# Attention and two gated layers on one core: a planner that knows the port of DVE and POOL, attention outputs on halves of PE's columns, and an opening time for the second chunk's attention

## The chip, the cores and the metric

One core of a Trainium2 chip. The time is that of one launch on the device, in microseconds (us). The engines are PE (matrix products), ACT (scalar), DVE (vector), POOL (GpSimd) and SP (the queue from which the transfers are started). Each engine carries out its instructions in the order in which the program lists them for that engine.

## The reference, cut to what matters

Random-feature attention over 4 batches of 576 tokens and 8 heads of 64, then two gated layers of width 512 with 1536 hidden units, over all 2304 tokens:

```python
def phi(x):                      # x already scaled by 64 ** -0.25
    h = einsum('bhsd,md->bhsm', x, omega) - sum(x * x) / 2
    return exp(h - max(h)) / sqrt(128)
q_p, k_p = phi(q_s), phi(k_s)
kv = einsum('bhsm,bhsd->bhmd', k_p, v); z = sum(k_p, over tokens)
attn = einsum('bhsm,bhmd->bhsd', q_p, kv) / (einsum('bhsm,bhm->bhs', q_p, z) + 1e-6)
x = heads side by side                       # 2304 x 512
x = (silu(x @ w_gate) * (x @ w_val)) @ w_out       # first layer
x = ((x @ w_a) * (x @ w_b)) @ w_out2               # second layer
```

The kernel takes the weights as 64-bit floats and makes 32-bit ones of them.

## The kernel before, in words

The tokens are cut into five chunks (`spans`): chunks 0 to 3 of 512 and chunk 4 of 256. Heads go in pairs, p = 0 to 3. For each chunk c, `layer(c, 0)` and `layer(c, 1)` do the two gated layers, and beside them the attention of chunk c + 1 is done (`keys` and `queries`, lines 833 to 837), so that PE has both kinds of work to choose from. Chunk 0's attention comes alone, at the start.

In the layers each number x is split in two fp32r parts, a high one (made by ACT, an ACTIVATE copy) and a low one (DVE, `sub`, line 321: x minus the high part). A product of 128 x 128 weights with 512 tokens is three matmuls, lines 770, 771, 772: high x high, high weights x low tokens, low weights x high tokens. `weights` loads a tile of 128 x 512 weights; the first time it makes 32-bit floats of 64-bit ones with two ACT instructions (lines 729, 732) and two DVE instructions (lines 735, 738), and keeps the result in DRAM; each time ACT makes the high part `wh` (line 750) and DVE the low part `wl` (line 753, counted at line 321). `put` (line 528) turns a PSUM tile into the high and low parts `xh`, `xl` of a layer's input.

Attention. `features` (line 367) projects with omega, takes the maximum (DVE, line 453), and the exponential (ACT, line 465). The squares of the tokens are made by POOL (line 382), their sums by DVE (384, 387: `s`, `nsq`), and `top` and `bias` are DVE's too (456, 460). `how` says in which form: WHOLE (chunk 0, plain fp32), SPLIT (chunk 1, three fp32r matmuls, line 443), STACKED (chunks 2 to 4, line 418). Then chunks 0 and 1 take `own` (line 556): transposes (567), outputs with the denominator as a 65th column (587), a division on DVE (604, 608, 612: `xt`), transposes back (621), `put`. Chunks 2 to 4 take `shared` (line 627): denominators from POOL products (652) and DVE sums (659), POOL scales the features (669), PE transposes them for each head h (679), and then they are split: ACT makes `fh` (682), DVE `fl` (685, counted at 321). For each batch b that the chunk touches, ACT and DVE split the sums `kvs` of both heads into high and low parts in a tile `kp` (693, 696) that holds 64 columns of head 0, 64 zeros, 64 columns of head 1; POOL writes the zeros once (354). `attend` (line 700) does, for each head, three matmuls (705) with 128 columns of `kp`, half of them zeros, all six adding up in one PSUM tile. A chunk of 512 touches two batches (widths 128 and 384 in chunk 2, 320 and 192 in chunk 3), chunk 4 touches one: five calls for each head pair, 20 in all, 120 matmuls.

Order. No order is written by hand. Each operation is recorded with its engine, a cost (`pace` for how long it holds the engine, `lat` for when its result is there) and a due time (`on`, line 316; `act`, `dve`, `pool`, `pe`, `dma` are the costs). `Plan.order` (line 98) then plays a list schedule: at each step the engine that is free first takes, of its operations whose inputs and tiles are there, the one that is due first; the order in which they are taken is the order in which each engine's instructions are issued. An operation that is due late is taken early if its engine has nothing else ready. `slack` makes an engine's inputs later in the plan, `after` is an earliest time. Tiles come from rings (`Ring`): a tile is given out again when all operations on its last use are planned. Four tiles of the ring `zb` lie in the memory of `fT`, which `own` uses. The costs do not know of each other: an instruction of DVE costs the same whether POOL works beside it or not.

Of the kernel before, what the change touches and what calls it, by code (L numbers as in the profile page):

```python
# [16 lines left out]
P = 128  # L17
# [4 lines left out]
class Ring:  # L22


    def __init__(self, make, n, name):
        self.tiles = [make(f"{name}{i}") for i in range(n)]
        self.free = [(0.0, i) for i in range(n)]
        self.recorded = []
        self.next = 0
# [22 lines left out]
class Op:  # L52
    __slots__ = ("eng", "pace", "lat", "due", "fn", "table", "deps", "bufs", "users", "open",
                 "ready", "start", "end", "n", "size", "slack")


class Plan:

# [10 lines left out]
    RATE = 0.24  # L69

# [3 lines left out]
    def add(self, eng, pace, due, fn, reads=(), writes=(), lat=None, table=None, size=0.0, slack=0.0,  # L74
            after=0.0):
        o = Op()
        o.eng, o.pace, o.due, o.fn, o.table, o.size, o.slack = eng, pace, due, fn, table, size, slack
        o.lat, o.ready = pace if lat is None else lat, after
# [19 lines left out]
    def order(self):  # L98
# [11 lines left out]
        table, pipe, done = None, 0.0, []  # L110

# [21 lines left out]
        while True:  # L133
# [18 lines left out]
            pace, lat = o.pace, o.lat  # L152
            if o.table and o.table != table:
# [24 lines left out]
            for b in o.bufs:  # L178
                b.left -= 1
                b.end = max(b.end, o.end)  # L180
                if b.left == 0 and b.ring is not None:
                    b.ring.free.append((b.end, b.slot))
                    for x in held.pop(id(b.ring), []):
                        offer(x)
# [11 lines left out]
def attention_moe_moe(ctx: ExitStack, tc: tile.TileContext, qT, kT, q, k, v, omegaT,  # L196
# [23 lines left out]
    NT = 512  # L220
# [33 lines left out]
    zeros = Fixed(None)  # L254
# [21 lines left out]
    r_zb = ring("zb", 2, [P, 2, M])  # L276
    for i in range(NT // P):
        r_zb.free.append((0.0, len(r_zb.tiles)))
        r_zb.tiles.append(r_fT.tiles[0].rearrange("p h (t m) -> p (h t) m", m=M)[:, 2 * i:2 * i + 2])
    r_kp = ring("kp", 2, [P, 2, 3, D], F32R)  # L280
    r_fh = ring("fh", 2, [P, NT], F32R)
    r_fl = ring("fl", 2, [P, NT], F32R)
# [31 lines left out]
    slack = dict.fromkeys((PE, ACT, DVE, POOL, SP), 0.0)  # L314

    def on(eng, cost, due, fn, reads=(), writes=(), table=None, late=None, after=0.0):
        return plan.add(eng, due=due, fn=fn, reads=reads, writes=writes, table=table,
                        slack=slack[eng] if late is None else late, after=after, **cost)
# [8 lines left out]
    n_ffn = 3 * (2 * NF * KD + NF * KD)  # L327
    begin = [ALONE]
# [8 lines left out]
    def constants():  # L337
# [15 lines left out]
        for i, t in enumerate(r_kp.tiles):  # L353
            on(POOL, dict(pace=0.25), 60, lambda t=t: nc.gpsimd.memset(
                t[:, :, 1].bitcast(F32), 0.0), writes=[(zeros, i)], after=ALONE)
        on(DVE, dve(256), 30, lambda: nc.vector.tensor_copy(bdh.tile, bd.tile),
           reads=[(bd, *bd.state)], writes=[(bdh,)], after=ALONE / 2)
        on(DVE, dve(256), 30, lambda: sub(nc.vector, bdl.tile, bd.tile, bdh.tile),
# [8 lines left out]
    def features(rT, tok, nt, step, f, due, length, how, psum, first):  # L367
# [19 lines left out]
        on(DVE, dve(16), due - 2, lambda: nc.vector.tensor_scalar(  # L387
# [21 lines left out]
        for g in range(0, nt, 2):  # L409
# [46 lines left out]
            on(DVE, dve(4), d, lambda mx=mx, top=top, n=n, g=g: nc.vector.scalar_tensor_tensor(  # L456
# [3 lines left out]
            on(DVE, dve(4), d, lambda top=top, bias=bias, n=n, g=g: nc.vector.tensor_tensor(  # L460
# [166 lines left out]
    def shared(c, p, f, due, length):  # L627
# [9 lines left out]
        for g in range(0, nt, 2):  # L637
# [25 lines left out]
            on(DVE, dve(4), d, lambda g=g: nc.vector.tensor_scalar(  # L663
# [10 lines left out]
        for h in range(2):  # L674
            d = due + length * (0.5 + 0.2 * h)
            ps, fh, fl = ps_t.buf(), r_fh.buf(), r_fl.buf()
            turned.append((fh, fl))
            for t in range(nt):
# [3 lines left out]
            on(ACT, act(n, 0, True), d, lambda ps=ps, fh=fh: nc.scalar.activation(  # L682
                out=fh.tile[:, 0:n], in_=ps.tile[:, 0:n], func=AF.Copy),
                reads=[(ps, *range(nt))], writes=[(fh,)])
            on(DVE, dve(n), d, lambda ps=ps, fh=fh, fl=fl: sub(
                nc.vector, fl.tile[:, 0:n], ps.tile[:, 0:n], fh.tile[:, 0:n]),
                reads=[(ps, *range(nt)), (fh,)], writes=[(fl,)])
        ps = ps_t.buf()
        for b in batches:
            kp, kv = r_kp.buf(), sums[b, p]  # L690
            cols = slice(max(t0, b * S) - t0, min(t1, (b + 1) * S) - t0)
            width = cols.stop - cols.start
            on(ACT, act(2 * D), due + length * 0.3, lambda kp=kp, kv=kv: nc.scalar.activation(
                out=kp.tile[:, 0, 0:3:2], in_=kv.tile[:, :, 0:D], func=AF.Copy),
                reads=[(kv, 0), (zeros, *range(2))], writes=[(kp, 0)])
            on(DVE, dve(2 * D), due + length * 0.3, lambda kp=kp, kv=kv: sub(
                nc.vector, kp.tile[:, 1, 0:3:2], kv.tile[:, :, 0:D], kp.tile[:, 0, 0:3:2]),
                reads=[(kv, 0), (kp, 0), (zeros, *range(2))], writes=[(kp, 1)])
            for h in range(2):
                def attend(h=h, kp=kp, cols=cols):  # L700
                    (xh, xl), out = turned[h], ps.tile[:, cols]
                    hi, lo = (kp.tile[:, i].rearrange("p a d -> p (a d)")[:, D * h:D * h + P]
                              for i in range(2))
# [176 lines left out]
```

## Time and profile before

| what | us |
|---|---|
| median of 3 runs (lowest, highest) | 1060.49 (1054.83, 1061.13) |
| the profiled execution's own time | 1058.15 |
| its span, from first to last instruction | 1056.4 |
| busy time of PE | 1039.0 |
| busy time of DVE | 748.8 |
| busy time of ACT | 686.6 |
| busy time of POOL | 170.4 |

The profile is of one execution. Durations in it are of single instructions; a matmul's duration reaches past the start of the next one, so what matmuls cost in a row is read from the distance of their starts. An idle time is named with the engine that ended it.

### The profile page before, as it was taken

Reading aid. Unit: us, or ns where it says so; the run is one execution under the profiler, and the core shown is the slowest. Engines: PE = TensorE matmul, PEld = TensorE weight load, DVE = VectorE, ACT = ScalarE, POOL = GpSimd, SP = SyncE. Lnnn points to the kernel's source line nnn. Section 1 sums busy time; section 2 is a strip of 40 time slices with the busy share of each in tenths; the row PEclk is TensorE's granted clock in tenths of the full one; section 3 lists DMA queues with packets and bytes.
Section 4 is the critical chain, followed back from the end, with each engine's and each line's share of the span. In section 5 each row is a group of like instructions: output and inputs, shape, how many; then the busy total and the mean of one; then the engine's idle time right before and its main releaser. Section 6 shows DMA issues by size and latency. Waiting matters only on the chain.

```text
span 1056.4 us, 15912 instructions
## 1 busy us (share of the span) xinstructions
PE 1039.0 (98%) x5444; PEld 887.8 (84%) x5444; DVE 748.8 (71%) x1441; ACT 686.6 (65%) x1433; POOL 170.4 (16%) x148
## 2 busy tenths in 40 slices
PE   7989999999999999999999999999999999999998
PEld 6877888888888878888888888888888888889998
DVE  5989899999766698998544577775554365537663
ACT  5988788888666767887444567665564255437563
POOL 1321020220200042343200034223000011000000
PEclk9999999999999999999999999999999999999999
DMA  7856877687865465564433333333333332336663
GB/s 246 280 188 218 254 259 229 222 257 227 287 201 182 159 216 174 181 205 147 130 104 96 100 113 106 89 87 114 99 100 100 90 92 88 100 120 186 184 182 99
DMA packets 102768, 172.02 MB, mean 163 GB/s; under 512 B 9376, under 2 KB 42784, under 8 KB 102688
## 3 DMA queue, kind: packets, MB, share of 16 engines
q1 hardware_dynamic: 102608, 170.99, 52.0%
q8 instruction: 42, 0.69, 0.3%
q14 instruction: 38, 0.31, 0.1%
q10 hardware_dynamic: 80, 0.03, 0.0%
HBM read 147.39 MB, written 23.59 MB: 162 GB/s over the span
## 4 chain that ended last, share of the span: by engine, by line
PE 87%; DVE 7%; ACT 3%; issue 2%; DMA 1%; SPq 0%; DVEq 0%; ACTq 0%
PE ps_m L771 26%; PE ps_m L772 26%; PE ps_m L770 26%; PE ps_kv L497 3%; PE ps_p L418 2%; PE ps_p L443 1%; PE ps_t L705 1%; DVE w L738 1%; DVE wl L321 1%; PE ps_t L587 1%; DVE mx L453 1%; PE ps_t L679 1%; DVE w L735 1%; PE ps_m L443 1%; DVE h L791 0%
## 5 line engine op out<-in xcount | busy, mean ns | idle before, releaser
L321 DVE TENSOR_TENSOR wl<-w,wh 128x512 fp32r<-128x512 f32 x360 | 262.8, 734 | 170.3 <-ACT wh L750 164.3
L770 PE MATMUL ps_m<-xh,wh 128*128 128x512 f32 (+1 forms) x960 | 359.4, 374 | 1.5 <-ACT wh L750 0.8
L771 PE MATMUL ps_m<-xl,wh 128*128 128x512 f32 (+1 forms) x960 | 355.4, 370 | 2.9 <-DVE xl L321 2.9
L772 PE MATMUL ps_m<-xh,wl 128*128 128x512 f32 (+1 forms) x960 | 355.1, 370 | 0.0
L750 ACT ACTIVATE wh<-w 128x512 fp32r<-128x512 f32 x360 | 224.9, 629 | 129.5 <-PE ps_m L771 99.6
L772 PEld LDWEIGHTS ps_m<-xh,wl 128*128 128x128 f32 x960 | 181.8, 189 | 31.5 <-DVE wl L321 0.7
L771 PEld LDWEIGHTS ps_m<-xl,wh 128*128 128x128 f32 x960 | 181.7, 189 | 30.0 <-DVE xl L321 3.6
L770 PEld LDWEIGHTS ps_m<-xh,wh 128*128 128x128 f32 x960 | 181.8, 189 | 29.1 <-ACT wh L750 1.3
L770 PE MATMUL ps_m<-hh,wh 128*128 128x512 f32 (+1 forms) x480 | 180.8, 377 | 0.0
L772 PE MATMUL ps_m<-hh,wl 128*128 128x512 f32 (+1 forms) x480 | 177.3, 369 | 0.0
L771 PE MATMUL ps_m<-hl,wh 128*128 128x512 f32 (+1 forms) x480 | 177.2, 369 | 0.0
L321 POOL TENSOR_TENSOR rs<-xT,rs 64x576 fp32r<-64x576 f32 (+4 forms) x48 | 63.7, 1327 | 536.2 <-issue 203.7
L791 DVE TENSOR_TENSOR h<-a,ps_m 128x512 f32<-128x512 f32 (+1 forms) x120 | 75.5, 629 | 51.6 <-PE ps_m L772 42.4
L788 ACT ACTIVATE a<-ps_m 128x512 f32<-128x512 f32 (+1 forms) x120 | 66.3, 552 | 66.9 <-PE ps_m L772 66.5
L772 PEld LDWEIGHTS ps_m<-hh,wl 128*128 128x128 f32 x480 | 90.5, 189 | 15.6
L770 PEld LDWEIGHTS ps_m<-hh,wh 128*128 128x128 f32 x480 | 90.7, 189 | 12.5
L771 PEld LDWEIGHTS ps_m<-hl,wh 128*128 128x128 f32 x480 | 90.7, 189 | 12.0
L794 ACT ACTIVATE hh<-h 128x512 fp32r<-128x512 f32 (+1 forms) x120 | 70.6, 588 | 32.2 <-DVE h L791 30.1
L735 DVE SCALAR_TENSOR_TENSOR w<-w 128x512 uint32<-128x512 uint32 x108 | 78.1, 726 | 7.1 <-ACT w L732 6.8
L321 DVE TENSOR_TENSOR hl<-h,hh 128x512 fp32r<-128x512 f32 (+1 forms) x120 | 77.3, 644 | 6.1 <-ACT hh L794 2.7
L738 DVE SCALAR_TENSOR_TENSOR w<-w,w 128x512 uint32<-128x512 uint32 x108 | 78.0, 723 | 2.6 <-ACT w L729 2.5
L732 ACT ACTIVATE w<-w 128x512 uint32<-128x512 uint32 x108 | 72.5, 678 | 5.7 <-DMA w<-w 5.6
(92 smaller groups left out, 1055.1 us busy)
## 6 DMA issues: line engine op xcount, KB each, us to landing
w<-kept SPq DMA_DIRECT2D x252, 256.0 KB, 2.7
w<-w SPq DMA_DIRECT2D x108, 512.0 KB, 4.6
kept<-w SPq DMA_DIRECT2D x72, 256.0 KB, 4.5
kt<-k_t SPq DMA_DIRECT2D x16, 320.0 KB, 3.8
vt<-v_t SPq DMA_DIRECT2D x16, 320.0 KB, 4.6
xT<-kT SPq DMA_DIRECT2D x16, 288.0 KB, 4.0
qt<-q_t SPq DMA_DIRECT2D x16, 256.0 KB, 4.1
outT<-h SPq DMA_DIRECT2D x16, 256.0 KB, 2.1
```

Of the source, the lines that this page charges most:

```text
L321: eng.tensor_tensor(out=out, in0=a, in1=hi.bitcast(F32), op=ALU.subtract)
L497: nc.tensor.matmul(kv.tile[:, (P + 1) * h:(P + 1) * (h + 1)], lhsT=f.tile[0:r, t, h], rhs=vt.tile[0:r, t], start=(t == 0 and h == 0), stop ...
L732: on(ACT, act(CW), due - 10, lambda: nc.scalar.activation(out=raw.tile[:, :, 0], in_=raw.tile[:, :, 0], func=AF.Copy, scale=0.875 * 2.0 ** ...
L735: on(DVE, dve(CW), due - 9, lambda: nc.vector.scalar_tensor_tensor(out=raw.tile[:, :, 0], in0=raw.tile[:, :, 1], scalar=0x80000000, in1=ra ...
L738: on(DVE, dve(CW), due - 9, lambda: nc.vector.scalar_tensor_tensor(out=w.tile.bitcast(U32), in0=w.tile.bitcast(U32), scalar=3, in1=raw.til ...
L750: on(ACT, act(CW), due - 7, lambda: nc.scalar.activation(out=hi.tile.rearrange("p a c -> p (a c)"), in_=w.tile, func=AF.Copy), reads=[(w,) ...
L770: nc.tensor.matmul(o, lhsT=hi.tile[:, wi], rhs=a, start=first, stop=False)
L771: nc.tensor.matmul(o, lhsT=hi.tile[:, wi], rhs=b, start=False, stop=False)
L772: nc.tensor.matmul(o, lhsT=lo.tile[:, wi], rhs=a, start=False, stop=last)
L788: on(ACT, act(n, 0, True), due, lambda a=a, ps=ps: nc.scalar.activation(out=a.tile[:, 0:n], in_=ps[0].tile[:, 0:n], func=AF.Silu if m == 0 ...
L791: on(DVE, dve(n), due, lambda a=a, h=h, ps=ps: nc.vector.tensor_tensor(out=h.tile[:, 0:n], in0=a.tile[:, 0:n], in1=ps[1].tile[:, 0:n], op= ...
L794: on(ACT, act(n), due + 2, lambda h=h, hh=hh: nc.scalar.activation(out=hh.tile[:, 0:n], in_=h.tile[:, 0:n], func=AF.Copy), reads=[(h,)], w ...
```

## The change: what it does

Five edits.

- The planner gets a shared port for DVE and POOL (`HELD`). Operations marked `port=True` are all of POOL's that go by `pool` and those of DVE with two inputs in SBUF, and some small ones (`dve(n, True)`). When a marked operation's turn comes while the other engine holds the port, its planned pace and latency grow by the wait; DVE takes an unmarked operation instead if it has one. This changes planned times and so the order on every engine; the instructions of `weights`, `layer` and `features` stay as they are.
- `shared` no longer splits the features: ACT copies each head's transposed features to a plain fp32 tile `ft` (ring of 3), and DVE's `fl` goes. `kp` goes, with its zeros, its ACT and its DVE instructions.
- `attend` is one operation for both heads: an fp32 matmul for each head, with the 64 columns of that head's sums as weights and its output on partitions 0 to 63 or 64 to 127 of the PSUM tile. The planner's cost of it is new. `put` then waits for all batches' parts.
- `OPENS = 55.0`: the operations of chunk 1's attention on PE, ACT, DVE and POOL (not SP's loads) may start no earlier than 55 us in the plan.
- `r_zb`'s four tiles inside `fT` are free only once `fT` has had its last use in the plan (`heir`).

```diff
-    def dve(n, rate=1):
-        return dict(pace=0.07 + n / 960 / rate, lat=0.19 + n / 960 / rate)
+    def dve(n, port=False):
+        return dict(pace=0.07 + n / 960, lat=0.19 + n / 960, port=port)
     def pool(n):
-        return dict(pace=0.2 + n * 0.0023)
+        return dict(pace=0.2 + n * 0.0023, port=True)
...
+    HELD = {DVE: (1.0, 0.1), POOL: (0.75, 0.0)}
...
+            if o.port:
+                wait = port[POOL if e == DVE else DVE] - t
+                if wait > 0 and e == DVE:
+                    other = [x for x in q if not x[2].port]
+                    if other:
+                        x = min(other)
+                        q.remove(x)
+                        heapq.heapify(q)
+                        heapq.heappush(q, (o.due, o.n, o))
+                        o = x[2]
+                        pace, lat = o.pace, o.lat
+                if o.port:
+                    wait = max(0.0, wait)
+                    share, less = self.HELD[e]
+                    pace, lat = pace + wait, lat + wait
+                    port[e] = t + wait + share * o.pace - less
...
+                    if r.heir and r.used == len(r.recorded):
+                        to, slots = r.heir
+                        to.free += [(b.end, i) for i in slots]
...
-                        slack=slack[eng] if late is None else late, after=after, **cost)
+                        slack=slack[eng] if late is None else late, after=max(after, opens[eng]),
+                        **cost)
...
+    OPENS = 55.0
...
+            opens.update(dict.fromkeys((PE, ACT, DVE, POOL), OPENS if c == 0 else 0.0))
...
-            on(ACT, act(n, 0, True), d, lambda ps=ps, fh=fh: nc.scalar.activation(
-                out=fh.tile[:, 0:n], in_=ps.tile[:, 0:n], func=AF.Copy),
-                reads=[(ps, *range(nt))], writes=[(fh,)])
-            on(DVE, dve(n), d, lambda ps=ps, fh=fh, fl=fl: sub(
-                nc.vector, fl.tile[:, 0:n], ps.tile[:, 0:n], fh.tile[:, 0:n]),
-                reads=[(ps, *range(nt)), (fh,)], writes=[(fl,)])
+            on(ACT, act(n, 0, True), d, lambda ps=ps, ft=ft: nc.scalar.activation(
+                out=ft.tile[:, 0:n], in_=ps.tile[:, 0:n], func=AF.Copy),
+                reads=[(ps, *range(nt))], writes=[(ft,)])
...
-            on(ACT, act(2 * D), due + length * 0.3, lambda kp=kp, kv=kv: nc.scalar.activation(
...
-            on(DVE, dve(2 * D), due + length * 0.3, lambda kp=kp, kv=kv: sub(
...
-                    for j, (w, x) in enumerate(((hi, xh), (hi, xl), (lo, xh))):
-                        nc.tensor.matmul(out, lhsT=w, rhs=x.tile[:, cols], start=h + j == 0,
-                                         stop=h == 1 and j == 2)
-                on(PE, pe(3 * max(0.12, FFN * width)), due + length, attend,
-                   reads=[(kp, 0, 1), *((x,) for x in turned[h])], writes=[(ps,)])
+            def attend(kv=kv, cols=cols):
+                for h in range(2):
+                    nc.tensor.matmul(
+                        ps.tile[h * D:(h + 1) * D, cols], lhsT=kv.tile[:, h, 0:D],
+                        rhs=turned[h].tile[:, cols], start=True, stop=True)
+            on(PE, pe(max(0.26, 4 * FFN * width) + 0.3 / len(batches)), due + length, attend,
+               reads=[(kv, 0), *((ft,) for ft in turned)], writes=[(ps, b)])
```

## Rows read from the trace of the kernel before

**Rows 1.** The page, first part: busy us of each engine (share), instructions.

```profile
PE 1039.0 (98%) x5444; PEld 887.8 (84%) x5444; DVE 748.8 (71%) x1441; ACT 686.6 (65%) x1433; POOL 170.4 (16%) x148
```

**Rows 2.** What PE waited for: us in total, times, longest us.

```profile
PE ps_m L771 <- DVE xl L321: 2.9, 2, 2.4
PE ps_t L621 <- DVE xt L612: 1.9, 1, 1.9
PE ps_m L770 <- ACT wh L750: 0.8, 1, 0.8
PE ps_p L418 <- DVE qf L429: 0.7, 1, 0.7
...
PE ps_m L770 <- ACT xh L532: 0.7, 1, 0.7
```

**Rows 3.** Stretches: us, busy of each engine (instructions), granted clock, DMA share, GB/s.

```profile
59.80:63.20 3.40, 3.28 (x8) 2.56 (x9) 1.69 (x6) 3.23 (x6) 0.00 (x0) 0.50 0.71 227
...
80.00:100.00 20.00, 19.17 (x85) 15.52 (x84) 19.66 (x31) 16.28 (x30) 4.15 (x2) 1.00 0.70 229
...
150.00:250.00 100.00, 100.00 (x544) 85.53 (x543) 97.34 (x198) 84.34 (x178) 15.37 (x9) 1.00 0.74 234
...
397.70:401.10 3.40, 3.40 (x12) 2.82 (x12) 2.26 (x5) 2.92 (x8) 0.00 (x0) 0.50 0.69 186
```

**Rows 4.** Timeline of PE at the start: start us, us, instruction, [idle before].

```profile
54.06 0.36 PE L443 MATMUL ps_p<-bdh,rs 128*128 128x256 f32 x1
...
55.54 0.38 PE L621 MATMUL ps_t<-ident,xt 128*128 128x128 f32 x2
...
58.97 0.51 PE L770 MATMUL ps_m<-xh,wh 128*128 128x512 f32 x1 [0.69 <-ACT xh L532]
```

**Rows 5.** Timeline of DVE, start of the kernel.

```profile
45.60 1.23 DVE L387 TENSOR_SCALAR nsq<-s 128x8 f32<-128x8 f32 x1
...
55.16 1.64 DVE L735 SCALAR_TENSOR_TENSOR w<-w 128x512 uint32<-128x512 uint32 x1
...
56.81 0.65 DVE L453 TENSOR_REDUCE mx<-ps_p 128x4 f32<-128x512 f32 x1
```

**Rows 6.** Timeline of POOL, start of the kernel.

```profile
45.55 1.25 POOL L382 TENSOR_TENSOR kt<-kt 128x640 f32<-128x640 f32 x1
...
55.00 1.25 POOL L382 TENSOR_TENSOR kt<-kt 128x640 f32<-128x640 f32 x1 [2.25 <-DMA kt<-k_t]
```

**Rows 7.** Timeline of DVE around the start of chunk 1's second layer.

```profile
391.64 1.52 DVE L735 SCALAR_TENSOR_TENSOR w<-w 128x512 uint32<-128x512 uint32 x1
...
396.00 0.68 DVE L321 TENSOR_TENSOR xl<-ps_m,xh 128x512 fp32r<-128x512 f32 x1
```

**Rows 8.** Timeline of ACT, the same place.

```profile
392.29 0.58 ACT L532 ACTIVATE xh<-ps_m 128x512 fp32r<-128x512 f32 x1
```

**Rows 9.** The chain by time: attention outputs of chunks 2, 3, 4.

```profile
520.74 1.72 PE ps_t L705 x12
...
749.15 1.55 PE ps_t L705 x12
880.70 0.71 PE ps_t L705 x6
```

**Rows 10.** Timeline of PE: fp32 products of 256 columns, start of the kernel.

```profile
14.82 0.60 PE L443 MATMUL ps_m<-bd,xT 128*128 128x256 f32 x2
15.26 0.49 PE L567 MATMUL ps_t<-ident,qf 128*128 128x128 f32 x3
```

**Rows 11.** Timeline of PE: from a matmul of the layers to attention outputs.

```profile
748.77 0.39 PE L772 MATMUL ps_m<-xh,wl 128*128 128x512 f32 x1
748.99 0.25 PE L705 MATMUL ps_t<-fh,kp 128*128 128x192 f32 x1
```

**Rows 12.** Groups of instructions by line and shape: busy us, mean ns.

```profile
L321 DVE TENSOR_TENSOR fl<-ps_t,fh 128x512 fp32r<-128x512 f32 x16 | 10.3, 683 | 1.8 <-ACT fh L682 1.8
...
L387 DVE TENSOR_SCALAR nsq<-s 128x8 f32<-128x8 f32 x16 | 3.6, 226 | 0.0
```

More of the change, by code (lines that the diff above doesn't have):

```diff
@@ L25, in __init__ @@
     def __init__(self, make, n, name):
-        self.tiles = [make(f"{name}{i}") for i in range(n)]
+        self.tiles, self.name = [make(f"{name}{i}") for i in range(n)], name
         self.free = [(0.0, i) for i in range(n)]
         self.recorded = []
-        self.next = 0
+        self.next = self.used = 0
+        self.heir = None
     def buf(self):
@@ L53 @@
     __slots__ = ("eng", "pace", "lat", "due", "fn", "table", "deps", "bufs", "users", "open",
-                 "ready", "start", "end", "n", "size", "slack")
+                 "ready", "start", "end", "n", "size", "slack", "port")
 class Plan:
@@ L74, in add @@
     def add(self, eng, pace, due, fn, reads=(), writes=(), lat=None, table=None, size=0.0, slack=0.0,
-            after=0.0):
+            after=0.0, port=False):
         o = Op()
         o.eng, o.pace, o.due, o.fn, o.table, o.size, o.slack = eng, pace, due, fn, table, size, slack
+        o.port = port
         o.lat, o.ready = pace if lat is None else lat, after
@@ L110, in order @@
         table, pipe, done = None, 0.0, []
+        port = {DVE: 0.0, POOL: 0.0}
         def offer(o):
@@ L181, in order @@
                 if b.left == 0 and b.ring is not None:
-                    b.ring.free.append((b.end, b.slot))
-                    for x in held.pop(id(b.ring), []):
+                    r = b.ring
+                    r.free.append((b.end, b.slot))
+                    r.used += 1
+                    again = held.pop(id(r), [])
+                    if r.heir and r.used == len(r.recorded):
+                        to, slots = r.heir
+                        to.free += [(b.end, i) for i in slots]
+                        again += held.pop(id(to), [])
+                    for x in again:
                         offer(x)
@@ L253, in attention_moe_moe @@
     ones = Fixed(None)
-    zeros = Fixed(None)
     ident = fixed("ident", [P, P])
@@ L276, in attention_moe_moe @@
     r_zb = ring("zb", 2, [P, 2, M])
+    r_fT.heir = (r_zb, range(len(r_zb.tiles), len(r_zb.tiles) + NT // P))
     for i in range(NT // P):
-        r_zb.free.append((0.0, len(r_zb.tiles)))
         r_zb.tiles.append(r_fT.tiles[0].rearrange("p h (t m) -> p (h t) m", m=M)[:, 2 * i:2 * i + 2])
-    r_kp = ring("kp", 2, [P, 2, 3, D], F32R)
-    r_fh = ring("fh", 2, [P, NT], F32R)
-    r_fl = ring("fl", 2, [P, NT], F32R)
+    r_ft = ring("ft", 3, [P, NT])
     r_den = ring("den", 3, [P, NT // P, 2])
@@ L314, in attention_moe_moe @@
     slack = dict.fromkeys((PE, ACT, DVE, POOL, SP), 0.0)
+    opens = dict.fromkeys((PE, ACT, DVE, POOL, SP), 0.0)
     def on(eng, cost, due, fn, reads=(), writes=(), table=None, late=None, after=0.0):
         return plan.add(eng, due=due, fn=fn, reads=reads, writes=writes, table=table,
-                        slack=slack[eng] if late is None else late, after=after, **cost)
+                        slack=slack[eng] if late is None else late, after=max(after, opens[eng]),
+                        **cost)
     def sub(eng, out, a, hi):
@@ L352, in constants @@
                 t[:, :, 2 * D:2 * D + 1], 1.0), writes=[(ones, i)])
[L353 to L356, printed above, removed]
+        on(DVE, dve(256, True), 30, lambda: nc.vector.tensor_copy(bdh.tile, bd.tile),
            reads=[(bd, *bd.state)], writes=[(bdh,)], after=ALONE / 2)
-        on(DVE, dve(256), 30, lambda: sub(nc.vector, bdl.tile, bd.tile, bdh.tile),
+        on(DVE, dve(256, True), 30, lambda: sub(nc.vector, bdl.tile, bd.tile, bdh.tile),
            reads=[(bd, *bd.state), (bdh,)], writes=[(bdl,)])
@@ L386, in features @@
             op=ALU.add, axis=AX.X), reads=[(tok,)], writes=[(s,)])
-        on(DVE, dve(16), due - 2, lambda: nc.vector.tensor_scalar(
+        on(DVE, dve(16, True), due - 2, lambda: nc.vector.tensor_scalar(
             out=nsq.tile[:, 0:nt], in0=s.tile[:, 0:nt], scalar1=sq_scale, scalar2=None,
@@ L752, in weights @@
             reads=[(w,)], writes=[(hi,)])
-        on(DVE, dve(CW), due - 6, lambda: sub(
+        on(DVE, dve(CW, True), due - 6, lambda: sub(
             nc.vector, lo.tile.rearrange("p a c -> p (a c)"), w.tile,
@@ L796, in layer @@
                 reads=[(h,)], writes=[(hh,)])
-            on(DVE, dve(n), due + 2, lambda h=h, hh=hh, hl=hl: sub(
+            on(DVE, dve(n, True), due + 2, lambda h=h, hh=hh, hl=hl: sub(
                 nc.vector, hl.tile[:, 0:n], h.tile[:, 0:n], hh.tile[:, 0:n]),
@@ L838, in attention_moe_moe @@
             slack.update({PE: 0.0})
+            opens.update(dict.fromkeys(opens, 0.0))
         layer(c, 1)
```

26 lines of the change are left out of this document (9 added, 17 removed).

## The prediction

> **What bounds the kernel now.** I read the page first. PE is busy 1039.0 of a span of 1056.4 us, 98%, DVE 71%, ACT 65%, POOL 16% [rows 1]. So PE is the bound over the whole, and only two things can shorten the kernel: less work on PE, or less of PE's idle time. All of that idle time is 1056.4 - 1039.0 = 17.4 us, and part of it lies before the first operands land and after the last matmul, which nothing here touches.
>
> Next the waits of PE, to see which idle times the change can reach [rows 2]. At the end of chunk 0's attention: 1.9 us for `xt`, 0.7 for `xh`, and the smaller of the two waits for `xl`, 2.9 - 2.4 = 0.5. At the start of chunk 1's second layer: 2.4 for `xl`. Besides, 0.8 for `wh` and 0.7 for `qf`. Together 7.0 us.
>
> Then the stretches, for the clock and for DVE [rows 3]. Behind the first and the third of these holes stand 3.4 us with a granted clock of 0.50, the lower level, 1.2 GHz (at full speed it is 2.4); PE had been idle just before each. In 3.4 us at half clock PE does 1.7 us of work, so each hole costs 1.7 us more than its wait. DVE is nearly full between 80 and 100 us (19.66 of 20) and between 150 and 250 (97.34 of 100): an average of 71% hides that chunk 0's stage has hardly any of DVE left.
>
> Last the timelines around the two holes. At the start, PE does projections of chunk 1 from 54.06 on, because it has nothing else, and comes back to the layers at 58.97 [rows 4]. On DVE a 128 x 8 `nsq` takes 1.23 us at 45.60, and L735 takes 1.64 us at 55.16 [rows 5]; over these POOL squares tokens (1.25 us from 45.55, and from 55.00) [rows 6]. An undisturbed DVE instruction of 512 elements takes 0.68 [rows 7], and `nsq` takes 0.23 in the mean [rows 12]. In both cases DVE ends about when POOL does, so one waits for the other, and the planner of before has no cost for this.
>
> **The change part by part.** The sum is made against the profiled execution's own time, 1058.15; the median of the three runs, 1060.49, is 2.3 us above it.
>
> *The opening time.* The second square, the `mx` at 56.81 and the projections at 54.06 belong to chunk 1; so does the first square, since the keys of chunk 0's last head pair were squared before. Held back, they free DVE ahead of `xt`: 1.23 - 0.23 = 1.0 from `nsq`, 1.64 - 0.68 = 0.96 from L735, 0.65 from `mx`, together 2.6. PE comes back to the layers at about 56.4. But the projections from 54.06 to 55.54 filled the hole with 1.48 us of work that PE now does later, where nothing is free: 2.6 - 1.5 = 1.1 gained. The hole that is left is about as long as the one of before (3.1 idle, minus 2.6, plus 1.5, so 2.0), and the lower clock may follow it or not. I take half of 1.7: 0.85. Ends: nothing on DVE gained and the filler lost, +1.5; all gained, -1.1 - 1.7 = -2.8. I take -1.95.
> What is moved with them: POOL's squares and low parts and ACT's high parts go later, and nothing of chunk 0 stands behind them. SP's loads have no opening time, but a token load needs the tile that the held-back `s` frees, so loads of the next head pair go later too; a load that is issued where its tile isn't free yet would hold up the weight loads behind it on SP. The plan issues it when its plan says the tile is free, so I cost it at nothing; where the cover is gone it shows as waits for `w`.
> All of it falls on DVE and POOL after 55 us. Between 150 and 250 us DVE has 2.7 us to spare and around 90 us 0.3 [rows 3]; the due times of chunk 1's attention lie from 114 us on, so most can go where DVE has room. Cost nothing, in the worst case a rival (below).
>
> *The planner's port.* Not one instruction of the layers goes; only the order changes. At the hand-over to chunk 1's second layer `xl` starts at 396.00 and ends at 396.68, which ends PE's 2.4 us wait, so PE stood from 394.28. Its input `xh` was there at 392.29 + 0.58 = 392.87 [rows 8], and the L735 that DVE was in, 1.52 us long, ended at 393.16 [rows 7]. Had `xl` come right behind it, it would have ended at 393.84, ahead of PE's need. Instead other instructions stood before it, as in the plan DVE was further on. A plan that carries such waits has `xl` ready nearer to where it is, and `xl` has an early due time. So I take the wait and its clock stretch as gone: -2.4 - 1.7 = -4.1; ends 0 and -4.1. By the same reason the 0.7 for `qf`: ends 0 and -0.7, taken whole, as the work that goes (below) comes from the same stretch. Of the 0.8 for `wh`, in a stretch where DVE stays full, half: -0.4 (ends +1.0, by the 1.0 us that one more square costs DVE, and -0.8). The planner can't take the port away; where a new hole opens, it costs what these did.
>
> *`fl`, `kp` and their zeros gone.* DVE loses a subtraction of 0.68 us for each head and chunk [rows 12], and for each of the 20 calls `kp` on ACT and on DVE. Neither engine bounds chunks 3 and 4, so that is worth nothing there; in chunk 2's attention it is part of why I take the two waits above as gone. POOL's two memsets: nothing. `ft` is the copy that `fh` was, at its price.
>
> *The outputs.* Before, twelve matmuls of a head pair in chunk 2 hold PE 1.72 us, in chunk 3 1.55, the six in chunk 4 0.71 [rows 9]: four times each, 4 x 3.98 = 15.9. After, each call has two fp32 matmuls. An fp32 product of 256 columns, recorded as two matmuls, holds PE from 14.82 to 15.26 = 0.44 us [rows 10], so 512 columns 0.88. One head after the other: 1.76, 1.76 and 0.88 a head pair, 4 x 4.40 = 17.6, +1.7. Both heads side by side all the time: half of it, 8.8, -7.1. The trace has no matmul on half of the columns, so these are the ends. Inside one product the two recorded matmuls follow one another in rows 10, and both need the same columns; so head 0's second can at best run beside head 1's first, three steps in place of four: 13.2, -2.7. I take -2.7. The calls become one for both heads and so wait for the later head's `ft`; PE has the layers' matmuls meanwhile, cost nothing.
> The Trainium skill (TensorE: Matmul & The Clock Gate, Measured speedup) gives three column tiles 2.38 times the speed; for two halves fully side by side the sum would be 7.1 less instead of 2.7. No run here shows it yet.
>
> *`heir`.* Chunk 2's attention, which takes the four tiles, comes long after `own`'s last use of `fT`: nothing.
>
> Sum: -1.95 - 4.1 - 0.7 - 0.4 - 2.7 = -9.85, so 1048.3.
>
> **The rivals.**
> *One head after the other.* The halves don't overlap: +1.7 for -2.7, so 1052.7. For: nothing in this trace runs two matmuls at once. Against: they use different columns.
> *The holes stay.* The list schedule is greedy, and a better clock in it need not move `xl`: without the 4.1, the 0.7 and the 0.4, 1053.5; if also the first hole stays, 1055.5. For: the plan's other errors (weights' loads, exponentials) stay. Against: both holes have a POOL instruction on the DVE instruction before them.
> *Draining at each change of form: slower.* A matmul of the layers lasts 0.39 us though the next one starts 0.22 after it [rows 11]. If PE had to empty itself before and after each of the 20 calls, since they use the array in another form than the layers, that is up to 40 x 0.39 = 15.6 us, and the heads then stand one after the other, +1.7. With the other terms (-7.15) kept, 1058.15 + 17.3 - 7.15 = 1068.3. It decides from (7.15 - 1.7) / 40 = 0.14 us a change on; with only the tail of 0.39 - 0.22 = 0.17 it would be 1059.5.
> The Trainium skill (TensorEngine Tiling (Array Packing), Key Properties) states that a change of the tiling mode drains the engine, which is what this rival is made of; no row of before shows such a change. Against it in the rows: the switch from 512 columns to L705's 192 costs nothing extra (0.22), but that is no change of form.
> *Everything side by side, all holes closed.* -2.8 - 4.1 - 0.7 - 0.8 - 7.1 = -15.5, 1042.7.
> *DVE full in chunk 0.* The work held back meets a DVE that is full from 150 to 250: the 2.6 us come back as PE waits, the sum is 1050.9. It is inside the range.
>
> **How the numbers follow.** Forecast with its own range of 1044 to 1053, 0.62 (the DVE case in it); one head after the other 0.12; holes stay 0.12; everything 0.08; draining 0.06. The range takes in both ends of the outputs and of the holes, 1042.7 and 1055.5, and 2.5 to 3 us more on each side, since one execution of before lies 2.3 us off the median: 1040 to 1059. About 1% is what a measurement of this kernel can tell from no change; 1% below 1058.15 is 1047.6, just under the forecast. Of its 0.62 a little under half lies beyond, 0.30, with everything's 0.08 gives faster 0.38. Slower by over 1% needs 1068.7, only the upper end of draining: 0.04. The rest, 0.58, is within 1%.
>
> **What would show it.** Right: PE's first lasting run of layer matmuls starts at 56 to 57 us; no wait for `xl` at the start of chunk 1's second layer and no half clock behind it; `nsq` and L735 without POOL beside them before 56; the outputs of a head pair hold PE some 1.3 us (0.7 in chunk 4). Wrong: a new wait of PE of 2 us or more between 60 and 300 for `wh`, `wl` or `w`; outputs at 1.8 us, or the layer's matmul behind them starting late; the hole at the start as long as before with the clock down.

## The result, and the profile after

The changed kernel takes 1049.34 us (median of 6 runs, 1048.85 to 1049.90). The kernel before, timed beside it on the same chip and in the runs shown ahead, takes 1058.81 (1054.83 to 1063.47 over all its runs in this study). The ratio is 0.9916, with a 95% interval of 0.9899 to 0.9934: some 0.8% faster. The forecast was 1048.3, with a range of 1040 to 1059. The profiled execution after took 1049.24, its span is 1047.1.

The page's first part of the changed kernel, for [rows 1]:

```profile
PE 1034.0 (99%) x5404; PEld 873.1 (83%) x5404; DVE 726.6 (69%) x1397; ACT 682.1 (65%) x1413; POOL 167.0 (16%) x146
```

PE's busy time fell by 5.0 us (1039.0 to 1034.0) and its idle time from 17.4 to 13.1. What PE waited for, for [rows 2], behind a wait for the first operands as before:

```profile
...
PE ps_m L787 <- ACT a L805: 1.1, 2, 0.7
PE ps_kv L524 <- ACT kf L492: 0.7, 1, 0.7
PE ps_m L787 <- ACT xh L559: 0.7, 1, 0.7
PE ps_m L788 <- DVE xl L350: 0.6, 3, 0.2
...
PE ps_t L648 <- DVE xt L639: 0.2, 1, 0.2
PE ps_p L445 <- DVE qf L456: 0.2, 1, 0.2
```

The 1.9 for `xt` is 0.2, the 2.4 for `xl` is gone (the longest of three is 0.2), the 0.8 for `wh` doesn't stand among them any more, that for `qf` is 0.2. New are 1.1 for `a`, ACT's first step behind the layers' matmuls. The stretches behind the two holes, and the two full ones, for [rows 3]:

```profile
55.90:59.30 3.40, 2.42 (x10) 1.69 (x10) 2.96 (x4) 3.37 (x6) 2.90 (x2) 1.00 0.41 156
80.00:100.00 20.00, 20.00 (x90) 16.54 (x89) 19.84 (x36) 16.01 (x29) 5.63 (x2) 1.00 0.78 252
150.00:250.00 100.00, 100.00 (x545) 86.00 (x544) 96.94 (x202) 85.09 (x179) 12.12 (x9) 1.00 0.73 236
391.00:394.40 3.40, 3.23 (x18) 2.41 (x17) 3.18 (x8) 1.56 (x5) 0.00 (x0) 1.00 0.13 43
```

Where before 3.4 us of half clock followed each hole, the granted clock is 1.00. DVE is as full between 80 and 100 and between 150 and 250 us as it was. PE at the end of chunk 0's attention, for [rows 4], and POOL, before and after, for [rows 6]:

```profile
53.48 0.39 PE L789 MATMUL ps_m<-xh,wl 128*128 128x512 f32 x1
53.71 0.38 PE L648 MATMUL ps_t<-ident,xt 128*128 128x128 f32 x2
54.32 0.44 PE L648 MATMUL ps_t<-ident,xt 128*128 128x128 f32 x2 [0.23 <-DVE xt L639]
55.45 0.49 PE L787 MATMUL ps_m<-xh,wh 128*128 128x512 f32 x1 [0.69 <-ACT xh L559]
```

```profile
41.36 1.41 POOL L321 TENSOR_TENSOR rs<-xT,rs 128x576 fp32r<-128x576 f32 x1 [7.47 <-ACT rs L403]
42.73 1.04 POOL L382 TENSOR_TENSOR qt<-qt 128x512 f32<-128x512 f32 x1
```

```profile
36.77 1.04 POOL L409 TENSOR_TENSOR qt<-qt 128x512 f32<-128x512 f32 x1
...
43.11 1.25 POOL L409 TENSOR_TENSOR kt<-kt 128x640 f32<-128x640 f32 x1 [4.07 <-DMA kt<-k_t]
56.05 1.46 POOL L350 TENSOR_TENSOR rs<-xT,rs 128x576 fp32r<-128x576 f32 x1 [11.68 <-ACT rs L430]
```

PE does layer matmuls up to the last transposes, and comes back for good at 55.45 in place of 58.97. On POOL the square of chunk 1's first keys is still made at 43.11, before 55. The opening time is one of the plan, not a wait: it puts the operation later in POOL's list, and POOL, with nothing ahead of it in that list, starts when the data is there. Chunk 1's low parts `rs` (made by POOL's `sub`) did move, from 41.36 to 56.05. Before, the square of chunk 0's last queries (`qt`, 42.73) stood behind them on POOL; after, it comes at 36.77. DVE at the start of chunk 1's second layer, for [rows 7], and the outputs in the chain by time, for [rows 9]:

```profile
390.54 0.93 DVE L755 SCALAR_TENSOR_TENSOR w<-w,w 128x512 uint32<-128x512 uint32 x1
391.39 0.68 DVE L350 TENSOR_TENSOR xl<-ps_m,xh 128x512 fp32r<-128x512 f32 x1
```

```profile
513.55 1.01 PE ps_t L720 x8
...
740.38 1.04 PE ps_t L720 x8
...
901.92 0.58 PE ps_t L720 x4
```

The stages, each by the first matmul of a chunk's first layer in the two traces (L770 before, L787 after, counted by number), in us from the span's start:

| | chunk 0 complete | chunk 1 | chunk 2 | chunk 3 | chunk 4 | last matmul of that line |
|---|---|---|---|---|---|---|
| before | 58.97 | 288.38 | 519.22 | 744.91 | 949.29 | 1052.61 |
| after | 55.45 | 284.65 | 509.99 | 734.00 | 939.74 | 1043.05 |
| gained so far | 3.5 | 3.7 | 9.2 | 10.9 | 9.6 | 9.6 |

("Chunk 0 complete" is the tenth product, the first that needs the last head pair.) So 3.5 us come from the start, 5.5 from chunk 1's stage, in which chunk 2's attention lies, and almost nothing from there on. The 10.9 falls to 9.6 again behind the last outputs of chunk 3, where PE waits 0.2 us for `xl` (at 742.82) and 0.3 for `a` (at 745.27); before, it waited for nothing there.

### The profile page after: what moved, and what is told of

It reads as the page before. It is cut to its first block, busy times and chain, and to the rows that moved or that the text cites. A ratio compares the mean times of both kernels' runs of the same rounds, so it can differ in the third digit from the quotient of the medians.

```text
span 1047.1 us, 15760 instructions
## 1 busy us (share of the span) xinstructions
PE 1034.0 (99%) x5404; PEld 873.1 (83%) x5404; DVE 726.6 (69%) x1397; ACT 682.1 (65%) x1413; POOL 167.0 (16%) x146
## 4 chain that ended last, share of the span: by engine, by line
PE 90%; DVE 4%; ACT 3%; DMA 2%; issue 1%; SPq 0%; DVEq 0%; ACTq 0%
PE ps_m L787 26%; PE ps_m L789 26%; PE ps_m L788 26%; PE ps_kv L524 3%; PE ps_p L445 2%; PE ps_p L470 1%; PE ps_t L614 1%; DMA w<-w 1%; PE ps_t L720 1%; PE ps_t L706 1%; PE ps_m L470 1%; DVE wl L350 1%; DMA kept<-w 1%; PE ps_t L594 1%; DVE w L755 1%
## 5 line engine op out<-in xcount | busy, mean ns | idle before, releaser
L787 PE MATMUL ps_m<-xh,wh 128*128 128x512 f32 (+1 forms) x960 | 359.1, 374 | 1.9 <-ACT a L805 1.1
L787 PEld LDWEIGHTS ps_m<-xh,wh 128*128 128x128 f32 x960 | 181.2, 189 | 32.6 <-issue 2.5
L787 PE MATMUL ps_m<-hh,wh 128*128 128x512 f32 (+1 forms) x480 | 181.3, 378 | 0.0
L787 PEld LDWEIGHTS ps_m<-hh,wh 128*128 128x128 f32 x480 | 90.7, 189 | 14.1 <-issue 1.3
L350 DVE TENSOR_TENSOR hl<-h,hh 128x512 fp32r<-128x512 f32 (+1 forms) x120 | 80.4, 670 | 8.0 <-ACT hh L811 4.9
```

The lines of the kernel that those rows point to most:

```text
L350: eng.tensor_tensor(out=out, in0=a, in1=hi.bitcast(F32), op=ALU.subtract)
L787: nc.tensor.matmul(o, lhsT=hi.tile[:, wi], rhs=a, start=first, stop=False)
```

## The experiments

Three edits make eight kernels, with each edit made or not; six of them are runs below. O is the outputs, A the opening time, P the planner's port. Of the other six kernels two measure the outputs, three the planner's rule, one the opening time. Each was timed beside the kernel before, whose median was 1057.8 to 1058.8 us there; differences from the changed kernel are of medians and good to about 1 us.

**Outputs alone (O).** The kernel before with `ft`, the new `attend`, and no `fl`, `kp`.

```diff
-            on(DVE, dve(n), d, lambda ps=ps, fh=fh, fl=fl: sub(
...
+                        ps.tile[h * D:(h + 1) * D, cols], lhsT=kv.tile[:, h, 0:D],
+                        rhs=turned[h].tile[:, cols], start=True, stop=True)
```

> The kernel before with only the new outputs (fp32 on halves of the columns, no split of features and sums), old planner, no opening time. Theory A (three separate gains: outputs on PE some 3 us, hand-over to chunk 1's second layer 4 to 5 us from the planner's port, start some 3.5 us): about 3 us under before, 1055 to 1056.5, and the wait of about 2.4 us for xl at the hand-over is still there. Theory B (the hand-over's gain comes from the DVE work that goes with fl and kp, not from the planner): 7 to 8 us under before, about 1051, wait gone.

1057.62, ratio 0.9990 (0.9977 to 1.0002). Neither theory: less than A's 3 us, far from B's 8. Its waits of PE from 290 to 525 us:

```profile
PE ps_p L412 <- DVE qf L423: 3.2, 2, 2.6
PE ps_m L755 <- DVE xl L318: 1.1, 1, 1.1
```

The wait for `xl` at the hand-over is 1.1 in place of 2.4, and another of 2.6 us is there, for `qf` in chunk 2's attention. DVE relieved of `fl` and `kp` does not close the hole; a shifted order moves it.

**The change without the port (O, A).** The rule is never taken.

```diff
-            if o.port:
+            if False:
                 wait = port[POOL if e == DVE else DVE] - t
```

> The changed kernel without the planner's port (marks stay, the rule is never taken); outputs and opening time as changed. Theory A: the wait for xl at the hand-over is back with its half clock, 4 to 5 us over the changed kernel, 1053 to 1055. Theory B: same as the changed kernel within 1 us.

1058.07, ratio 0.9994 (0.9978 to 1.0009): 8.7 us over the changed kernel, twice what was expected. The outputs and the opening together are worth nothing without the rule. In the same stretch:

```profile
PE ps_p L445 <- DVE qf L456: 2.8, 2, 2.1
```

The wait for `xl` at the hand-over, which theory A wanted back, is 0.4; the hole is again one for `qf`. It isn't all of the loss: chunk 0's stage is 4.0 us longer than in the changed kernel (table below). The profiled execution took 1055.78, 2.3 under the median.

**The change without the opening (O, P).**

```diff
-    OPENS = 55.0
+    OPENS = 0.0
```

> The changed kernel with the opening time set to 0. Theory A: squares of chunk 1 stand beside DVE again before 56 us and PE takes chunk 1's projections at the end of chunk 0's attention; PE comes back to the layers for good 2 to 4 us later: 2 to 4 us over the changed kernel, 1051.5 to 1053.5. Theory C (the planner's port alone keeps chunk 1's work out of the way): within 1 us of the changed kernel.

1051.88, ratio 0.9935 (0.9917 to 0.9954): 2.5 us over the changed kernel, as theory A had it. The tenth product starts at 57.17, behind the projections of chunk 1, and PE does not wait at the end of chunk 0's attention: without the opening, too, the hole at the start is closed. PE's waits from 56 to 290 us stand at 80 us, and the half clock behind them:

```profile
PE ps_m L789 <- DVE wl L350: 1.4, 1, 1.4
PE ps_m L787 <- ACT wh L767: 0.8, 1, 0.8
```

```profile
82.60:86.00 3.40, 3.40 (x10) 2.63 (x9) 3.40 (x7) 3.38 (x9) 1.11 (x1) 0.51 0.97 255
```

DVE and ACT are both full there. With the opening these waits are gone, and 0.2, 0.7 and 0.2 at the start and 0.7 for `a` behind it stand in their place.

**The change with the outputs of before (A, P).**

```diff
-                        ps.tile[h * D:(h + 1) * D, cols], lhsT=kv.tile[:, h, 0:D],
...
+                        nc.tensor.matmul(out, lhsT=w, rhs=x.tile[:, cols], start=h + j == 0,
+                                         stop=h == 1 and j == 2)
```

> The changed kernel with the outputs of before (fp32r parts of features and sums, six matmuls on all columns), planner's port and opening time as changed. Theory A: about 3 us over the changed kernel, 1052 to 1053, all of it in the stretches of the attention of chunks 2 and 3. Theory B: 6 us or more over it, with the wait at the hand-over back, as fl and kp load DVE there again.

1052.22, ratio 0.9936 (0.9916 to 0.9956): 2.9 us over the changed kernel, as A had it. B falls: the hand-over stays closed with `fl` and `kp` there.

**Opening alone (A).**

```diff
+            opens.update(dict.fromkeys((PE, ACT, DVE, POOL), 55.0 if c == 0 else 0.0))
```

> The kernel before with only the opening time of 55. So far: the new outputs alone gave 1 us, opening and outputs together without the port 0.5 us, as new waits for qf came in chunk 2's attention. Theory A (each edit's gain stands by itself): the layers go on 2.5 us earlier at the start and the rest is as before, 1055 to 1056.5. Theory D (only a plan that knows the port keeps gains; without it a shifted order opens another hole): within 1.5 us of before, 1057 to 1060, with the gain at the start visible and lost by the end of chunk 1.

1063.23, ratio 1.0048 (1.0032 to 1.0064): 5.1 us slower than before, beyond both theories. The tenth product starts at 55.99, 3.0 us earlier than before, chunk 1 at 290.14, 1.8 later. Then, from 290 to 525 us, and with the stretch of the long wait and the one behind it:

```profile
PE ps_p L420 <- DVE qf L431: 3.6, 1, 3.6
PE ps_m L773 <- DVE xl L323: 1.2, 1, 1.2
```

```profile
457.20:460.90 3.70, 0.07 (x1) 0.08 (x1) 3.68 (x7) 2.86 (x7) 0.00 (x0) 1.00 0.70 232
460.90:464.30 3.40, 3.40 (x9) 2.75 (x10) 3.40 (x5) 1.62 (x5) 2.92 (x2) 0.50 0.96 278
```

PE stands for 3.6 us, then has half the clock for 3.4. So the start's gain is there and is paid back, first in chunk 0's stage (1.3 us for `a` at 60, 1.3 for `wh` at 97, 1.0 for `qf` at 230), then by a hole in chunk 2's attention. DVE is busy for 39.5 of the 40 us from 60 to 100, but it is so in the changed kernel too: a full DVE alone doesn't make these waits.

**Port alone (P).** The planner's rule, its marks and `heir` in the kernel before; no opening.

```diff
+            if o.port:
+                wait = port[POOL if e == DVE else DVE] - t
...
-        on(DVE, dve(256), 30, lambda: nc.vector.tensor_copy(bdh.tile, bd.tile),
+        on(DVE, dve(256, True), 30, lambda: nc.vector.tensor_copy(bdh.tile, bd.tile),
```

> The kernel before with only the planner's port; outputs as before, opening time 0. Theory A and D: the hole at the hand-over to chunk 1's second layer goes, the start gains little: 3 to 5 us under before, about 1054 (the changed kernel plus 2.5 for the opening and 2.9 for the outputs gives 1054.8). If the port needs the other edits: within 1 us of before.

1053.18, ratio 0.9957 (0.9941 to 0.9973): 5.0 us faster by itself. From 290 to 525 us PE waits no more than this:

```profile
PE ps_t L552 <- DVE fl L353: 0.3, 1, 0.3
PE ps_p L451 <- DVE qf L462: 0.2, 1, 0.2
```

The start is 1.1 us earlier (57.84), and here too PE does not wait there. The page's first part of this run:

```profile
PE 1037.8 (99%) x5444; PEld 887.1 (84%) x5444; DVE 747.1 (71%) x1441; ACT 690.0 (66%) x1435; POOL 173.9 (17%) x148
```

DVE, with the same 1441 instructions, is busy 747.1 us, against 748.8 before. The rule hardly shortens what DVE's instructions take beside POOL; it changes what PE finds ready meanwhile.

**Both heads on one half.** Leaves the second half of the columns unwritten.

```diff
-                        ps.tile[h * D:(h + 1) * D, cols], lhsT=kv.tile[:, h, 0:D],
+                        ps.tile[0:D, cols], lhsT=kv.tile[:, h, 0:D],
```

> The changed kernel with both heads' outputs on the first 64 partitions; leaves the other half of the outputs' columns unwritten. If the heads run side by side in the changed kernel: the products go one after another, twice the streaming time, 8 x 0.85 + 4 x 0.43 = 8.5 us more, about 1058. If, as the prediction took, one step in four is shared: 17.6 / 4 = 4.4 us more, about 1054. If nothing is shared in the changed kernel: no change.

1057.71, 8.4 us over the changed kernel: the price of no sharing, 8.5 expected for heads that ran side by side. The eight recorded matmuls of a head pair, and what follows them:

```profile
402.15 1.94 PE L720 MATMUL ps_t<-ft,kvs 128*64 128x128 f32 x8
404.02 0.50 PE L787 MATMUL ps_m<-xh,wh 128*128 128x512 f32 x1
```

404.02 - 402.15 = 1.87 us, in place of 1.01 in the changed kernel (below).

**Each output product twice.**

```diff
-                for h in range(2):
+                for h in (0, 1, 0, 1):
```

> The changed kernel with every output product made twice within its call (same values). Adds products but no further changes of form. Side by side all the time: 8.8 us more, about 1058, and what the calls hold PE for beyond twice 0.85 (0.43 in chunk 4) is the price of the change of form. Three steps in place of four: 13.2 us more, about 1062.5. One after the other: 17.6 more, about 1067.

1057.93, 8.6 us over the changed kernel. In the chain by time a head pair of chunk 2 and one of chunk 4:

```profile
515.27 1.88 PE ps_t L720 x16
...
839.99 1.01 PE ps_t L720 x8
```

1.88 against 1.01 in the changed kernel, and in chunk 4 1.01 against 0.58 (834.29 - 833.71 in its timeline). So the second set of products adds 0.87 us for 512 columns and 0.43 for 256. That is half of the 1.76 and the 0.88 that [rows 10] give for two products one after the other: they run side by side all the time. The Trainium skill (TensorE: Matmul & The Clock Gate, Measured speedup vs the span model) gives 2.38 times the speed for three column tiles of 32; the trace agrees in kind, with 1.76 / 0.87 = 2.0 for two of 64. The changed kernel's timeline of PE around one call shows what is added:

```profile
401.61 0.39 PE L789 MATMUL ps_m<-xh,wl 128*128 128x512 f32 x1
401.93 1.08 PE L720 MATMUL ps_t<-ft,kvs 128*64 128x128 f32 x8
402.94 0.50 PE L787 MATMUL ps_m<-xh,wh 128*128 128x512 f32 x1
403.29 0.40 PE L788 MATMUL ps_m<-xl,wh 128*128 128x512 f32 x1
```

A layer matmul follows the one before it by 0.23, so the first output could have started at 401.84; it starts at 401.93. Layers go on at 402.94, and the second matmul there comes 0.35 behind the first, 0.12 more than usual. From 401.84 to 402.94, and 0.12: 1.22 us, 0.87 of it products, 0.35 for the change of form there and back. In chunk 4 it is 0.78 by the same reading, 0.43 and again 0.35. The Trainium skill (TensorEngine Tiling (Array Packing), Key Properties) states that changing the tiling mode drains TensorE; the trace agrees, with 0.35 us for the two changes. That it is the form, and not the change from fp32r to fp32, is seen where fp32 products on all columns stand between layer matmuls:

```profile
49.50 0.40 PE L789 MATMUL ps_m<-xh,wl 128*128 128x512 f32 x1
49.74 2.00 PE L614 MATMUL ps_t<-kvs,fT 128*128 128x65 f32 x16
51.55 0.47 PE L787 MATMUL ps_m<-xh,wh 128*128 128x512 f32 x1
51.86 0.40 PE L788 MATMUL ps_m<-xl,wh 128*128 128x512 f32 x1
```

They start 0.24 behind the layer matmul, so without the late start, and all that is lost there is about 0.1 us: 2.36 from the first row to the last, less 1.81 of products and two steps of 0.23. The form of the outputs is seen in the groups by shape, where 128*64 stands for rows and columns of the array:

```profile
L720 PE MATMUL ps_t<-ft,kvs 128*64 128x384 f32 x16 | 3.3, 486 | 0.0
```

**Wait costs without the choice.** The planner adds the waits but DVE takes no other operation instead.

```diff
-                    other = [x for x in q if not x[2].port]
+                    other = []
```

> The changed kernel, its planner still adding the wait for the port to the cost, but DVE no longer takes an unmarked operation instead. If the gain of the port (8.7 us with the other two edits) is that planned times are nearer to the real ones: within 2 us of the changed kernel, 1049 to 1051. If it is that DVE works on something else while POOL holds the port: 1055 to 1058.

1050.10, ratio 0.9919 (0.9898 to 0.9940), within 1 us of the changed kernel. The gain is in the planned times, not in DVE's choice. Whether the waits of DVE or those of POOL have to be in them was not tested. From 290 to 525 us the two longest waits are:

```profile
PE ps_m L787 <- ACT a L805: 0.6, 1, 0.6
PE ps_p L445 <- DVE qf L456: 0.4, 1, 0.4
```

**A mean cost instead of the port.** No rule; marked operations of DVE cost 0.06 us more.

```diff
+        more = 0.06 if port else 0.0
-        return dict(pace=0.07 + n / 960, lat=0.19 + n / 960, port=port)
+        return dict(pace=0.07 + n / 960 + more, lat=0.19 + n / 960 + more, port=port)
```

> The changed kernel without the port rule; instead each marked DVE operation costs 0.06 us more in the plan, about what the 360 subtractions for wl take over an undisturbed one in the mean (0.734 against 0.68). If it is enough that the plan's DVE is as slow as the real one in the mean: within 2 us of the changed kernel. If the plan has to know where the waits fall: as without the port, 1056 to 1059.

1051.20 (1048.13 to 1052.15), ratio 0.9922 (0.9898 to 0.9947). Within the 2 us of the first expectation; but in chunk 1's stage:

```profile
PE ps_p L446 <- DVE qf L457: 3.3, 2, 2.7
```

The hole is there as in the plans without the rule, though without half clock behind it. The start is 1.1 us earlier than in the changed kernel (tenth product at 54.38), but chunk 1 starts at 286.49, 1.8 later, and chunk 2 at 514.59, 4.6 later. So beside the other two edits most of the 8.7 us came back with the hole in place: the hole is not all that the rule is worth there. The same cost without the other edits follows.

**Mean cost alone.** The edit of the run above in the kernel before (with `heir`).

```diff
+        more = 0.06 if port else 0.0
-        return dict(pace=0.07 + n / 960 / rate, lat=0.19 + n / 960 / rate)
+        return dict(pace=0.07 + n / 960 + more, lat=0.19 + n / 960 + more, port=port)
```

> The kernel before with only a higher cost of DVE in the plan: each marked DVE operation costs 0.06 us more; no port rule, no opening, outputs as before. If a plan whose DVE is nearer to the real one in the mean is what the port rule gave: most of the 5 us that the port alone gave, 1053 to 1055.5. If the good time of the mean cost beside the other two edits was the luck of one order: within 1.5 us of before, 1056.5 to 1060.

1061.59, ratio 1.0038 (1.0022 to 1.0054): 3.8 us slower than before, beyond both expectations, and the waits of PE from 290 to 525 us are

```profile
PE ps_p L452 <- DVE qf L463: 4.7, 2, 3.0
PE ps_m L805 <- DVE xl L354: 0.7, 1, 0.7
```

A dearer DVE in the mean is not what the rule gives; its good time beside the other edits did not carry over.

**Opening at 65.**

```diff
-    OPENS = 55.0
+    OPENS = 65.0
```

> The changed kernel with the opening time at 65 instead of 55. If any time past the end of chunk 0's attention does (and DVE has room later): within 1 us of the changed kernel. If the held-back work runs into a DVE that is full up to 250 us: 1 to 4 us over it, with waits of PE between 100 and 290 us.

1053.41, ratio 0.9951 (0.9932 to 0.9970), 4.1 us over the changed kernel. Tenth product at 55.44, chunk 1 at 289.85. PE's largest wait from 56 to 290 us:

```profile
PE ps_m L787 <- ACT wh L767: 4.4, 2, 2.5
```

The two waits end at 108.82 and 126.33. Between them ACT is full and DVE is not:

```profile
108.80:126.30 17.50, 14.63 (x64) 11.71 (x64) 11.79 (x21) 17.36 (x27) 0.00 (x0) 1.00 0.59 190
```

So the work held back makes PE wait before 250 us, as the second expectation had it, but `wh` comes late with ACT busy 17.36 of 17.50 us and DVE 11.79; the start's gain is spent before chunk 1.

**The eight kernels together** (ratio to before, as timed beside it):

| | without O | with O |
|---|---|---|
| neither | 1 | 0.9990 |
| A | 1.0048 | 0.9994 |
| P | 0.9957 | 0.9935 |
| A and P | 0.9936 | 0.9916 |

The port gains in all four pairs: 0.0043, 0.0055, 0.0112 and 0.0078. The opening loses or does nothing without it (0.0048 slower, 0.0004) and gains 0.002 with it, in both pairs. The outputs gain 0.002 with the port, in both pairs; without it 0.001, and 0.005 beside the opening. A ratio is known to some 0.002, so a gain of 0.002 rests on the two pairs agreeing. Where the gains lie, by the starts of the stages in each trace, in us:

| | start (tenth product) | chunk 0's stage | chunk 1's stage |
|---|---|---|---|
| before | 59.0 | 229.4 | 230.8 |
| A | 56.0 | 234.2 | 233.5 |
| O | 58.9 | 229.9 | 231.1 |
| O and A | 56.1 | 233.2 | 228.0 |
| P | 57.8 | 230.0 | 226.6 |
| A and P | 55.9 | 229.3 | 227.6 |
| O and P | 57.2 | 230.2 | 225.3 |
| all three | 55.4 | 229.2 | 225.3 |

The rule shortens chunk 1's stage in every pair, by 2.7 to 5.9 us. It shortens chunk 0's stage, by 4 to 5 us, only where the opening stands, and there it undoes what the opening costs.

## Why the prediction was right

*The bound and the places.* The reading of the bound held: PE is 99% busy, and the gain came from less work on PE and from the holes that were named, though not each from the edit that was to close it. Of its signs of being right, the outputs (1.22 and 0.78 for 1.3 and 0.7) and the closed hand-over came; of those of being wrong one came in part, the layers' matmuls behind the outputs, of which the second is 0.12 late.

*The outputs, -2.7.* Measured: from 1.72, 1.55 and 0.71 to 1.22, 1.22 and 0.78 a head pair, 4 x (3.98 - 3.22) = 3.0, and 2.9 by the run with the old outputs. The sum was right by luck; the step to it was not. The prediction took one step in four as shared, since a product's two recorded matmuls need the same columns. In fact the heads run side by side all the time (the run with everything twice), which alone would give the 7.1 of its low end; and 12 times 0.35 = 4.2 us go back to the changes of form. The draining rival was right that a change of form costs PE time, at about 0.17 a change the tail that it named, but at 24 changes instead of 40, since the two calls of a head pair stand together; that the heads then stand one after the other was wrong.

*The hand-over, -4.1, and the 0.7 for `qf`.* Chunk 1's stage gained 5.5. With 4 x (1.72 - 1.22) = 2.0 of outputs in it, 3.5 are left for these 4.8; the rule alone shortens that stage by 4.2. The wait and its half clock did go; what of the rest was lost to another order isn't told apart. The cause named, plan times of DVE without the waits for POOL, is what the runs support: the six plans without the rule (before, O, A, O with A, and the two with the mean cost) each have one wait of PE of 2.1 to 3.6 us in chunk 1's stage, the six with it none over 0.8. It isn't `heir`, which three of the six plans without the rule have too. "The work that goes" was not needed: P alone closes the hole with `fl` and `kp` there, and A, which takes no work from DVE, shortens the wait for `xl` to 1.2, as O does to 1.1. The 1.7 of half clock for each hole does not always come: it follows the 2.6 and the 3.6 us of O and A, and not the 2.1 of O with A nor the 2.7 and 3.0 of the two with the mean cost (granted clock 1.00 behind them).

*The start, -1.95.* On top of the rule the opening is worth 0.002, some 2 us, as forecast, but that is luck. It was to shorten the hole at the end of chunk 0's attention; the rule alone closes that hole (no wait there in P and in O with P). Of the 3.5 us at the start, the rule alone gives 1.1, and the opening 1.7 to 2.0 more, 1.4 of which are projections that are moved to later (57.84 - 56.43 in P). What it takes away besides are the waits at 80 us with their half clock. Without the rule it does act as forecast: in A the layers go on 3.0 us earlier and the wait for `xt` is 0.8 in place of 1.9. After, the layers go on at 55.45, not 56.4, and PE waits 0.2, 0.7 and 0.2 there; the granted clock stays at 1.00, where half of a stretch at half clock was counted. The step on the filler was right in kind, but layer matmuls fill part of the place. "Held back" was wrong for POOL's first square, which is still made at 43.11, and "nothing of chunk 0 stands behind them" was wrong too: the square of chunk 0's last queries stood behind chunk 1's `rs` on POOL. With that square at 36.77, `nsq` stands at 41.20, before the square at 43.11, and takes 0.14 us. And the step took the edit as worth something by itself: alone it is 5 us slower. The rival "DVE full in chunk 0" counted 2.6 us of new waits and left them inside the range; without the rule chunk 0's stage is 4.8 longer, and at 65 it is 5.2 longer than in the changed kernel, there with ACT as the full engine.

*The 0.4 for `wh`.* Gone, and 0.7 for `a` came in the same stage.

*Two readings.* "In both cases DVE ends about when POOL does" holds for `nsq` (46.83 and 46.80); L735 ends at 56.80, 0.55 after POOL's square, with most of an undisturbed instruction's 0.68 still to come when POOL ended. That one waits for the other stands. And the range's upper end, 1059, is 3.5 us beyond 1055.5, not 2.5 to 3.

## What to carry to other kernels

Where a planner writes the order, what an engine waits for beyond the plan's costs is paid by the engine that bounds: put that wait into the plan where it falls, before tuning due times or earliest times against it; here an edit that frees the bound engine's start was 5 us slower on the old plan (and worth nothing there beside the new outputs) and 2 us faster on the better one. Halves of PE's columns are worth their change of form when enough products stand together: here the two changes cost 0.35 us, whether they enclosed 0.43 or 0.87 us of products, so that a head pair gained 0.50 and 0.33 us in chunks 2 and 3 and lost 0.07 in chunk 4.

## What was not expected of the hardware

Two fp32 products on different halves of the columns take the time of one: 0.87 us for 512 columns, side by side all the time, though each product is recorded as two matmuls that need the same columns.

The kernel before spread over 6.3 us in six runs (1054.83 to 1061.13), the changed kernel over 1.1 in six (1048.85 to 1049.90). The order is the same in all runs of a kernel. The mean granted clock goes along with it: over all runs of before it lies between 0.993 (in the slowest, 1063.47) and 1.000, in the changed kernel's six it is 0.999 or 1.000. That holes followed by half clock, or not, make the spread is only argued; no run here isolates it.
